# Head 0's projection, the warm products and TensorE's order in a masked attention, rewritten

## The chip, the cores and the metric

The kernel runs on one core of one Trainium2 chip. Its time is the device time of one execution in microseconds (us), and a version's time is the median of several executions. The engines are TensorE (PE; its loads of the stationary operand are listed apart as PEld), VectorE (DVE), ScalarE (ACT), GpSimd (POOL) and SyncE (SP), which here issues most of the transfers. Matrix products write to PSUM; the other engines copy from there to on-chip memory. Each engine runs its own instructions in the order in which they stand; between engines semaphores hold an instruction until what it reads is there.

## The reference

There are 2 batches of 8 heads, 768 positions, 64 numbers a head. A query and a key see each other only where the signs of their six projections agree.

```python
q_bits = (einsum('bhsd,dk->bhsk', q, proj) > 0)
k_bits = (einsum('bhsd,dk->bhsk', k, proj) > 0)
mask = bucket(q_bits)[:, :, :, None] == bucket(k_bits)[:, :, None, :]
scores = where(mask, q @ k.T / sqrt(64), -1e9)
attn = exp(scores - max(scores)); attn = attn / (sum(attn) + 1e-09)
x = attn @ v                                     # 1536 tokens x 512
h = maximum(maximum(x @ w1, x @ w2), x @ w3)     # 512 -> 768
y = h @ w_out                                    # 768 -> 512
z = y @ w_in                                     # 512 -> 2048
g = z if z >= 1 else 0 if z <= -1 else (z + 1)**2 / 4
out = g @ moe2_w_out                             # 2048 -> 512
```

## The kernel before

**The attention** takes the 16 heads (batch times head) in turn, each with six tiles of 128 queries by 768 keys, 96 tiles in all. A float32 number is held as a high part (`hi`) and the rest (`lo`), so that products of parts keep precision.

*Preparing a head.* The transposed keys and queries come into `r` (L309): 128 rows by 768 columns, keys above queries. One product per half, `bits_mm` (L389), gives the six projections of both; `bits_rows` (L395, VectorE) makes signs of them, which stand as 44 more rows in `qb`. `prep_scale` (L338) scales the queries, `prep_hi` and `prep_lo` split, and `prep_move` (L375) brings parts to other rows: `qa`, `qb`, `ql`, `kh`, `kb`. For the heads from the second on these moves are transfers issued by SyncE; `kb` needs the rows of the bits, `kh` needs `hi`. For head 0 they are copies by ScalarE and GpSimd in two halves of 384 columns, written out by hand in L596 to L621: the projection is scaled by three GpSimd ops (`pj_sign`, L327) to `pj_sc`, and 13 products of bf16 zeros, 128 x 256 (`warm_up`, L304), run on TensorE while the data are awaited. Four more stand in each half of tile 0 (L416).

*A tile.* `t_qk` (L407): for each half of the keys one product `qa` by `lo` (L414) and one of `qb` by `hi` (L417, 76 rows: the high parts and the bits, which push pairs of different buckets far down). `t_max` (L424, VectorE) takes the row maximum, `t_exp` (L439, ScalarE) the exponentials and their sums. There are two score buffers, `s_ps0` and `s_ps1`.

*The values.* For heads 0, 1, 3, 5, ... TensorE transposes each tile in 128 x 128 pieces (`t_tr`, L447, six a tile) into `t_ps`, `t_out` (L457) copies them, and `g_pv` (L508) multiplies three tiles with the values, a first third and then the rest. For the heads 2, 4, ... ("turned") VectorE transposes by 32 x 32 (`t_turn`, L464), and `block4` (L475) multiplies in four row quarters of the array, 96 products of 32 rows by 64 columns for each half of a head's blocks. `pair_rows` (L555) transposes the sums of two heads.

*The order.* Everything after head 0 is a task of a planner (`Work`, L43 to L110): a task has an engine, a cost, a due time, a lag and the tasks and buffers that it waits for, and the planner writes the instructions out in the order of its own model of time. For TensorE the order is laid down as a string (L828 to L838): `q` is the scores of a tile, `t` its transposes, `b` and `B` a head's bits, `v` and `w` the first and the rest of a value product (or the halves of a block product), `r` the sums, `m` two early pieces of the perceptrons. The number is the tile's place in the sequence (`SEQ`), not head times six plus tile: from head 1 on tiles of a turned head and another one alternate. `period`, twelve tiles, is repeated five times. Costs for changes of kind stand in L855 to L860. `SHIFT` (L630) moves the due times of the other engines' tasks.

**The perceptrons** follow from about 208 us to the end, three-part products as in `mm3` (L270) and L1017, with the weights' preparation on the other engines.

Of the kernel before, what the change touches and what calls it, by code (L numbers as in the profile page):

```python
# [8 lines left out]
F32 = mybir.dt.float32  # L9
# [104 lines left out]
def lsh_attention_moe_kernel(  # L114
# [33 lines left out]
    sc_sb = const.tile([128, 1], F32, name="sc_sb")  # L148
    one_exp = const.tile([128, 1], F32, name="one_exp")
# [131 lines left out]
    def attention(mlp_steps):  # L281
        with ExitStack() as ax, ExitStack() as sx:
# [24 lines left out]


# [98 lines left out]
            def t_qk(n, bank):  # L407
# [3 lines left out]
                for half in range(2):  # L411
# [3 lines left out]
                    if n == 0:  # L415
                        warm_up(4, half)  # L416
# [213 lines left out]
            SHIFT = {t_exp: 42.5, t_out: 2.0, g_copy: 17.5, copy4: -82.0, pair_copy: -20.5, w_tick: 60.0, bits_rows: 4.5, t_max: -12.5, t_turn: 8.0, pair_recip: 20.0}  # L630
# [9 lines left out]
            raw_s["prep"].free.pop()  # L640
            raw_s["r"].free.pop()

            def head_tasks(h):
# [17 lines left out]
                scaled[h], moves[h], r_place[h] = hi, [q, ql, kh], rp  # L661
                if h == 1:
                    bp = place("b", 1)
                    mm = task("PE", 0.644, due + 1, bits_both, h, after=[hi], takes=[bp], leaves=[rp])
# [36 lines left out]
            def tile_tasks(n):  # L701
# [6 lines left out]
                qk = task("PE", 0.72, m, t_qk, n, sp, after=ready[h], takes=[sp], leaves=[h_place[h]])  # L708
                mx = task("DVE", 1.04, m, t_max, n, sp, after=[qk], takes=[pp], leaves=[sp])
                ex = task("ACT", 1.13, m, t_exp, n, after=[mx], takes=takes, lag=0.1)  # L710
                exps[n] = ex
                order[f"qk{n}"] = [qk]
                if turned:
                    pt_p_[n] = place("dt", 1)
                    tu = task("DVE", 0.96, m - 1, t_turn, n, after=[ex] + outs.get(h, [])[-1:], takes=[pt_p_[n]], leaves=[pp])
                    outs.setdefault(h, []).append(tu)
                    return
# [5 lines left out]
                for half in range(2):  # L723
                    tr = task("PE", 0.288, m - 4, t_tr, n, half, after=[ex, tr], takes=[] if half else [tb], leaves=[pp], lag=0.1)
# [4 lines left out]
                    ways = [("ACT", 0.48 if alone else 0.76, nc.scalar.copy), ("DVE", 0.556 if alone else 0.955, nc.vector.tensor_copy)]  # L729
# [125 lines left out]
            for (x, a), (y, b_) in zip(line, line[1:]):  # L855
                b_["after"].append(a)
                if (x in "bp") != (y in "bp"):
                    b_["cost"] += 0.16
                elif x + y in ("qt", "qr", "bp", "pb"):
                    b_["cost"] += 0.06  # L860
# [238 lines left out]
```

## Time and profile before

| | us |
|---|---|
| median of 3 runs | 667.93 (667.04 to 668.33) |
| profiled execution, its own time | 668.48 |
| span of the profiled execution | 666.6 |
| busy in it: TensorE | 657.4 (99%) |
| VectorE | 486.2 (73%) |
| ScalarE | 341.0 (51%) |
| GpSimd | 274.4 (41%) |

The profile is one execution. Its own time lies 0.55 us above the median. A matrix product is listed with its line, the buffer that it writes, rows by columns of the array, its operand's shape and a count where like products are merged; the ends are modelled, so starts are what to compare. "Idle before" is the time in which the engine ran nothing, and the releaser is the instruction that ended it; "issue" stands where nothing that the profile shows was waited for.

### The profile page before, as it was taken

To read this page: it belongs to the slowest core of one execution; us is meant where nothing else is said; L and a number is where in the kernel's file an instruction comes from. 1 tells how busy PE (TensorE), PEld (TensorE's weight loads), DVE (VectorE), ACT (ScalarE), POOL (GpSimd) and SP (SyncE) were. 2 spreads that over 40 slices of the span, in tenths; PEclk is the share of its full clock that TensorE was granted. 3 is DMA by queue.
4 is the path that set the end of the run, shared out by engine and by line. 5 is a ranking of instruction groups with operands and counts; after the bars stand their busy time and mean duration, and the time that the engine had idled before them with its cause. 6 is when DMAs were issued, how large, how long until landed. Compare 5 with 4: busy or idle time off the path is not lost.

```text
span 666.6 us, 11523 instructions
## 1 busy us (share of the span) xinstructions
PE 657.4 (99%) x4419; PEld 527.4 (79%) x4419; DVE 486.2 (73%) x717; ACT 341.0 (51%) x633; POOL 274.4 (41%) x249
## 2 busy tenths in 40 slices
PE   8999999999999999999999999999999999999998
PEld 5667777777867888888888888888888888888886
DVE  5787989998863667875453466766888888888844
ACT  7787877887782233333222325665444444444430
POOL 5436556766322335344223113644444444444430
PEclk9999999999999999999999999999999999999999
DMA  6847787775243122322111122121111222211004
GB/s 194 221 122 185 199 217 197 186 243 140 83 135 81 64 95 72 119 70 65 47 49 56 55 73 86 42 71 57 63 64 64 63 65 63 64 63 64 32 0 190
DMA packets 27855, 66.99 MB, mean 100 GB/s; under 512 B 4164, under 2 KB 9124, under 8 KB 27800
## 3 DMA queue, kind: packets, MB, share of 16 engines
q1 hardware_dynamic: 27488, 66.21, 33.8%
q8 instruction: 35, 0.57, 0.4%
q14 instruction: 20, 0.16, 0.1%
q10 hardware_dynamic: 312, 0.04, 0.0%
HBM read 46.17 MB, written 3.19 MB: 74 GB/s over the span
## 4 chain that ended last, share of the span: by engine, by line
PE 96%; issue 1%; DVE 1%; DMA 1%; ACT 1%; SPq 0%; POOL 0%; POOLq 0%; DVEq 0%
PE b L270 49%; PE b L1017 20%; PE s_ps L414 6%; PE t_ps L447 5%; PE u_ps L508 5%; PE s_ps L417 5%; PE u_ps L475 3%; PE pj_ps L390 2%; PE t_ps L475 1%; DVE p L424 1%; DMA rb<-d 0%; PE pj_ps L475 0%; ACT p L439 0%; PE s_ps L270 0%; DMA d<-rt 0%
## 5 line engine op out<-in xcount | busy, mean ns | idle before, releaser
L270 PE MATMUL b<-x_hl,wx 128*128 128x512 f32 x684 | 159.6, 389 | 0.0
L270 PEld LDWEIGHTS b<-x_hl,wx 128*128 128x128 f32 x684 | 128.4, 188 | 26.6
L270 PE MATMUL b<-x_hl,w 128*128 128x512 f32 (+1 forms) x564 | 123.8, 376 | 0.0
L270 PEld LDWEIGHTS b<-x_hl,w 128*128 128x128 f32 x564 | 100.9, 188 | 19.8 <-issue 0.6
L917 POOL TENSOR_TENSOR g<-r,g 128x512 fp32r<-128x512 f32 x48 | 62.5, 1304 | 121.4 <-ACT g L916 121.4
L424 DVE TENSOR_SCALAR_CACHE_REDUCE p<-s_ps 128x768 f32<-128x768 f32 x96 | 89.7, 951 | 11.9 <-PE s_ps L417 8.7
L206 DVE SCALAR_TENSOR_TENSOR wg<-wg,wr 128x512 f32<-128x512 f32 (+1 forms) x58 | 67.3, 1160 | 37.6 <-ACT wg L204 36.9
L439 ACT ACTIVATE p<-p,nm 128x768 f32<-128x768 f32 x96 | 89.7, 936 | 5.6 <-DVE p L424 5.1
L414 PE MATMUL s_ps<-lo,q 128*128 128x384 f32 x192 | 72.0, 375 | 1.0 <-DVE p L424 0.9
L233 POOL TENSOR_TENSOR wx<-wg,wx 128x512 fp32r<-128x512 f32 (+1 forms) x32 | 45.6, 1426 | 65.3 <-ACT wx L227 48.4
L1017 PE MATMUL b<-wx,g 128*128 128x512 f32 x288 | 72.1, 389 | 0.0
L1017 PE MATMUL b<-w,g 128*128 128x512 f32 (+1 forms) x294 | 71.3, 385 | 0.0
L227 ACT CAST wx<-wg 128x512 fp32r<-128x512 f32 (+1 forms) x32 | 19.3, 604 | 92.6 <-DVE wg L219 92.6
L417 PE MATMUL s_ps<-hi,q 76*128 76x384 f32 x192 | 65.3, 340 | 0.0
L997 DVE SCALAR_TENSOR_TENSOR r<-r,b 128x512 f32<-128x512 f32 x48 | 33.0, 687 | 44.3 <-ACT r L996 44.3
L1017 PEld LDWEIGHTS b<-w,g 128*128 128x128 f32 x294 | 54.5, 188 | 11.1
L1017 PEld LDWEIGHTS b<-wx,g 128*128 128x128 f32 x288 | 54.1, 188 | 11.2
L1024 DVE TENSOR_TENSOR acc<-b,acc 128x512 f32<-128x512 f32 (+1 forms) x85 | 56.3, 675 | 7.7 <-PE b L1017 7.6
L233 POOL TENSOR_TENSOR w<-wg,w 128x512 fp32r<-128x512 f32 (+1 forms) x26 | 35.9, 1382 | 49.3 <-ACT w L227 39.1
L211 DVE TENSOR_SCALAR wg<-wg 128x512 int32<-128x512 int32 (+1 forms) x58 | 53.3, 920 | 2.7
L995 ACT ACTIVATE r<-b,half_sb 128x512 f32<-128x512 f32 x48 | 33.0, 687 | 41.3 <-PE b L270 41.3
L227 ACT CAST w<-wg 128x512 fp32r<-128x512 f32 (+1 forms) x26 | 15.8, 608 | 74.0 <-DVE wg L219 74.0
(90 smaller groups left out, 1060.2 us busy)
## 6 DMA issues: line engine op xcount, KB each, us to landing
wr<-in_w SPq DMA_DIRECT2D x48, 512.0 KB
r<-in_kq SPq DMA_DIRECT2D x15, 384.0 KB
q<-hi SPq DMA_DIRECT2D x15, 384.0 KB
v<-in_v SPq DMA_DIRECT2D x21, 256.0 KB
rb<-d SPq DMA_DIRECT2D x16, 192.0 KB
wr<-in_w SPq DMA_DIRECT2D x8, 384.0 KB
q<-lo SPq DMA_DIRECT2D x15, 192.0 KB
lo<-hi SPq DMA_DIRECT2D x15, 192.0 KB
```

Of the source, the lines that this page charges most:

```text
L206: nc.vector.scalar_tensor_tensor(out=f32(g), in0=f32(g), scalar=TINY_SQ, in1=f32(high), op0=ALU.is_ge, op1=ALU.mult)
L211: nc.vector.tensor_scalar(out=g2, in0=g, scalar1=3, scalar2=0x3FFFFFF8, op0=ALU.logical_shift_left, op1=ALU.bitwise_and)
L227: nc.scalar.copy(out=w[:, 0, 0:cols], in_=f32(g2))
L233: nc.gpsimd.tensor_tensor(out=w[:, 1, 0:cols], in0=f32(g2), in1=f32(w[:, 0, 0:cols]), op=ALU.subtract)
L270: nc.tensor.matmul(out=outp, lhsT=w_[a], rhs=x_[b_], start=(begins and i == 0 and jj == 0), stop=(ends and i == n - 1 and jj == 2),)
L414: nc.tensor.matmul(out=o, lhsT=hd["qa"][:, qs], rhs=hd["lo"][:, ks], start=True, stop=False)
L417: nc.tensor.matmul(out=o, lhsT=hd["qb"][0:76, qs], rhs=hd["hi"][0:76, ks], start=False, stop=True)
L424: nc.vector.tensor_scalar(out=p.rearrange("p (a k) -> p a k", a=2), in0=s_ps[bank.at][:, :, 0:HALF], scalar1=MASKED, scalar2=MASKED, op0=A ...
L439: nc.scalar.activation(out=p, in_=p, func=ACTF.Exp, scale=-1.0, bias=tl[n]["nm"], accum_out=sums_of(h // 2)[:, c:c + 1],)
L917: nc.gpsimd.tensor_tensor(out=dst[:, 1, cs], in0=src, in1=f32(dst[:, 0, cs]), op=ALU.subtract)
L1017: nc.tensor.matmul(out=pb[:, cs], lhsT=gs[f][:, a, tsl], rhs=wt[:, b_, cs], start=(n == 0), stop=(n == len(terms) - 1),)
L1024: nc.vector.tensor_tensor(out=acc[:, t, cs], in0=pb[:, cs], in1=acc[:, t, cs], op=ALU.add)
```

## The change

In the head: instead of 13 products of bf16 zeros, `warm_small(29)` puts 29 rounds of four float32 products of zeros, 32 rows by 64 columns out and 64 moving columns, one in each row quarter of the array, 116 in all. `pj_sc` comes from one GpSimd product of the raw projection with a table `pj_by`, which four memsets fill; `pj_sign` moves behind head 0 and is one op. The bits of head 0's two halves go to rows 0 to 63 of `pj_ps` and 64 to 127 of `u_ps`, one right behind the other; the copies of head 0 stand in a new order, and the second half of `qa` is made by GpSimd instead of ScalarE. In tile 0 one bf16 product stands in each half instead of four. In the attention: TensorE's strings are written anew, and the planner has other costs, lags, due times (`SHIFT`) and a table `SWITCH` for changes of kind; a head's bits wait for the scaled rows (`sc`) instead of `hi`.

```diff
+            def warm_small(rounds):
+                zeros = f32(warm)
+                for _ in range(rounds):
+                    for q in range(4):
+                        rows = slice(32 * q, 32 * q + 32)
+                        nc.tensor.matmul(
+                            out=quarter(q)[UP, HALF + 64:512], lhsT=zeros[rows, 0:64], rhs=zeros[rows, 64:128],
+                            start=True, stop=True,
+                        )
...
             def pj_sign():
-                for c0 in (0, 32):
-                    nc.gpsimd.tensor_scalar(
-                        out=pj_raw[:, c0:c0 + 6], in0=pj_raw[:, c0:c0 + 6], scalar1=-1.0, scalar2=0.0, op0=ALU.mult, op1=ALU.add
-                    )
-                nc.gpsimd.tensor_scalar(
-                    out=pj_sc, in0=pj_raw, scalar1=sc_sb, scalar2=0.0, op0=ALU.mult, op1=ALU.add
-                )
+                rows = pj_raw.rearrange("p (a b) -> p a b", a=2)[:, :, 0:6]
+                nc.gpsimd.tensor_scalar(out=rows, in0=rows, scalar1=-1.0, scalar2=0.0, op0=ALU.mult, op1=ALU.add)
...
                     if n == 0:
-                        warm_up(4, half)
+                        warm_up(1, half)
...
-            warm_up(13, 0)
+            warm_small(29)
             load_head(1)
             load_v(0)
-            banks0 = (pj_ps, u_ps)
             halves = [slice(0, HALF), slice(HALF, S)]
-            pj_sign()
-            prep_hi_scaled(0, halves[0])
-            bits_mm(0, 0, banks0[0], 64)
-            prep_lo_scaled(0, 0, nc.vector)
-            prep_move(0, "qb", nc.gpsimd.tensor_copy, halves[0])
-            prep_hi_scaled(0, halves[1])
-            bits_mm(0, 1, banks0[1], 64)
+            nc.gpsimd.tensor_tensor(out=pj_sc, in0=pj_raw, in1=pj_by, op=ALU.mult)
+            for half, bank in enumerate((pj_ps, u_ps)):
+                bits_mm(0, half, bank, 64 * half)
+                prep_hi_scaled(0, halves[half])
+            for half in range(2):
+                prep_move(0, "qb", nc.gpsimd.tensor_copy, halves[half])
+            prep_move(0, "qa", nc.gpsimd.tensor_copy, halves[1])
+            for half in range(2):
+                prep_lo_scaled(0, half, nc.vector)
             prep_move(0, "qa", nc.scalar.copy, halves[0])
             prep_move(0, "ql", nc.scalar.copy, halves[0])
-            prep_lo_scaled(0, 1, nc.vector)
             prep_move(0, "kh", nc.gpsimd.tensor_copy, halves[0])
-            bits_rows(0, 0, banks0[0], 64)
             prep_move(0, "ql", nc.scalar.copy, halves[1])
-            prep_move(0, "qb", nc.gpsimd.tensor_copy, halves[1])
-            prep_move(0, "qa", nc.scalar.copy, halves[1])
+            bits_rows(0, 0, pj_ps, 0)
             prep_move(0, "kh", nc.gpsimd.tensor_copy, halves[1])
             prep_move(0, "kb", nc.scalar.copy, halves[0])
-            bits_rows(0, 1, banks0[1], 64)
+            bits_rows(0, 1, u_ps, 64)
             prep_move(0, "kb", nc.scalar.copy, halves[1])
+            pj_sign()
...
+            SWITCH = dict(qt=0.095, qr=0.095, tq=-0.08, qp=0.17, qb=0.17, tp=0.094, tb=0.094)
...
-            SHIFT = {t_exp: 42.5, t_out: 2.0, g_copy: 17.5, copy4: -82.0, pair_copy: -20.5, w_tick: 60.0, bits_rows: 4.5, t_max: -12.5, t_turn: 8.0, pair_recip: 20.0}
+            SHIFT = {prep_scale_act: 10.0, prep_hi: 16.0, t_exp: 57.0, t_out: 13.0, g_copy: 18.5, copy4: -104.5, pair_copy: -48.0, w_tick: 68.0, bits_rows: 3.5, t_max: -45.0, t_turn: 6.5, pair_recip: -25.0}
...
-                scaled[h], moves[h], r_place[h] = hi, [q, ql, kh], rp
+                scaled[h], moves[h], r_place[h] = sc, [q, ql, kh], rp
...
             first_part = (
-                "q0 q1 B q2 t0 q3 q4 t1 t2 q5 b5 t3 v2 w2 t4 q6 q11 b8 t5 q7 q8 t6 v5 w5 q9 t7 q10 q12 t8 "
...
+                "q0 q1 B q2 t0 q3 t1 q4 q5 t2 b5 t3 v2 w2 t4 q6 q7 t5 b8 q8 q11 t6 q10 v5 t7 q9 w5 q12 t8 "
...
             period = (
-                "q22 q24 v19 w19 t21 q25 q26 v20 w20 q27 t23 q30 q28 t25 b25 q29 q35 t27 v25 w25 q31 r25 "
-                "t29 q32 b31 q33 t31 "
+                "q22 t19 q21 q24 v19 w19 t21 q25 q26 v20 w20 q27 t23 q28 q30 t25 q29 b25 q31 t27 v25 w25 "
+                "r25 t29 q35 q32 b31 "
             )
...
+        for rows, cols, by in ((slice(0, 64), 32, 1.0), (slice(64, 128), 0, SCALE)):
+            nc.gpsimd.memset(pj_by[rows], by)
+            nc.gpsimd.memset(pj_by[rows, cols:cols + 6], -by)
```

What this does to TensorE's row is shown at three places. In these rows a name ends in the number of its buffer, "x6" merges six like instructions, and the lines of the changed kernel are six to seven higher than those of the kernel before. The first place is the head, from the last warm products to tile 0 (`s_ps0`). Before:

```order
L306 LDWEIGHTS warm_82
L306 MATMUL t_ps_119<-warm_82 128x256
L390 MATMUL pj_ps_86<-r_120,pj_sc_77 64x384
L390 MATMUL u_ps_85<-r_120,pj_sc_77 64x384
L414 MATMUL s_ps0_116<-lo_145,q_146 128x384
L306 LDWEIGHTS warm_82
L306 MATMUL t_ps_119<-warm_82 128x256
L306 LDWEIGHTS warm_82
L306 MATMUL t_ps_119<-warm_82 128x256
```

Now:

```order
L314 MATMUL u_ps_86<-warm_83 64x64
L314 MATMUL t_ps_124<-warm_83 64x64 x2
L314 MATMUL pj_ps_87<-warm_83 64x64
L396 MATMUL pj_ps_87<-r_125,pj_sc_77 64x384
L396 MATMUL u_ps_86<-r_125,pj_sc_77 64x384
L420 MATMUL s_ps0_121<-lo_252,q_253 128x384
L307 LDWEIGHTS warm_83
L307 MATMUL t_ps_124<-warm_83 128x256
L423 MATMUL s_ps0_121<-hi_251,q_253 128x384
L420 MATMUL s_ps0_121<-lo_252,q_253 128x384
L307 LDWEIGHTS warm_83
L307 MATMUL t_ps_124<-warm_83 128x256
```

The two products of bits stand next to each other as before, but behind rounds of small products; one bf16 product is left behind each first score product.

The second place is TensorE's row in head 0, the transposes of tiles 1 and 2 (`p` is a tile's exponentials, `t_ps` the one buffer of transposes). Before:

```order
L414 MATMUL s_ps0_116<-lo_145,q_146 128x384
L417 MATMUL s_ps0_116<-hi_144,q_146 128x384
L414 MATMUL s_ps0_116<-lo_145,q_146 128x384
L417 MATMUL s_ps0_116<-hi_144,q_146 128x384
L447 MATMUL t_ps_119<-ident_84,p_198 128x128 x6
L447 MATMUL t_ps_119<-ident_84,p_213 128x128 x6
L414 MATMUL s_ps1_117<-lo_145,q_146 128x384
L417 MATMUL s_ps1_117<-hi_144,q_146 128x384
```

Now (from tile 2 in `s_ps0` on):

```order
L423 MATMUL s_ps0_121<-hi_251,q_253 128x384
L453 MATMUL t_ps_124<-ident_85,p_292 128x128 x6
L420 MATMUL s_ps1_122<-lo_252,q_253 128x384
L423 MATMUL s_ps1_122<-hi_251,q_253 128x384
L420 MATMUL s_ps1_122<-lo_252,q_253 128x384
L423 MATMUL s_ps1_122<-hi_251,q_253 128x384
L453 MATMUL t_ps_124<-ident_85,p_295 128x128 x6
L420 MATMUL s_ps0_121<-lo_252,q_253 128x384
L423 MATMUL s_ps0_121<-hi_251,q_253 128x384
```

The two rows of transposes stood in a row; now the scores of a tile stand between them.

The third place is TensorE's row around head 2's first scores (`lo_251` and `q_252` before, `lo_350` and `q_351` now; `lo_187` before and `lo_288` now are head 1's). Before:

```order
L447 MATMUL t_ps_119<-ident_84,p_329 128x128 x6
L508 MATMUL u_ps_85<-pt_293,vr_139 64x384 x6
L414 MATMUL s_ps0_116<-lo_187,q_188 128x384
L417 MATMUL s_ps0_116<-hi_186,q_188 128x384
L414 MATMUL s_ps0_116<-lo_187,q_188 128x384
L417 MATMUL s_ps0_116<-hi_186,q_188 128x384
L447 MATMUL t_ps_119<-ident_84,p_366 128x128 x6
L414 MATMUL s_ps1_117<-lo_251,q_252 128x384
L417 MATMUL s_ps1_117<-hi_250,q_252 128x384
```

Now:

```order
L453 MATMUL t_ps_124<-ident_85,p_430 128x128 x6
L420 MATMUL s_ps0_121<-lo_350,q_351 128x384
L423 MATMUL s_ps0_121<-hi_349,q_351 128x384
L420 MATMUL s_ps0_121<-lo_350,q_351 128x384
L423 MATMUL s_ps0_121<-hi_349,q_351 128x384
L514 MATMUL u_ps_86<-pt_392,vr_247 64x384 x2
L453 MATMUL t_ps_124<-ident_85,p_437 128x128 x6
L420 MATMUL s_ps1_122<-lo_288,q_289 128x384
L423 MATMUL s_ps1_122<-hi_287,q_289 128x384
L420 MATMUL s_ps1_122<-lo_288,q_289 128x384
L423 MATMUL s_ps1_122<-hi_287,q_289 128x384
L514 MATMUL u_ps_86<-pt_392,vr_247 64x384 x4
```

Head 2's first scores (q10) stood behind v5 and w5 (`u_ps`), q9 and t7; now they stand ahead of all of these.

## Rows read from the trace of the kernel before

**Rows 1.** Page, section 3 (DMA queue: packets, MB, share) and section 4 (longest chain).

```profile
q8 instruction: 35, 0.57, 0.4%
...
PE 96%; issue 1%; DVE 1%; DMA 1%; ACT 1%; SPq 0%; POOL 0%; POOLq 0%; DVEq 0%
```

**Rows 2.** Busy time by stage; columns: window, length, each engine, clock, DMA share, GB/s.

```profile
240.00:600.00 360.00, 360.00 (x1590) 298.20 (x1589) 254.76 (x324) 150.78 (x262) 135.62 (x101) 1.00 0.20 66
```

**Rows 3.** Timeline of TensorE in the head; columns: start, length, engine, line, instruction, count.

```profile
1.05 2.96 PE L306 MATMUL t_ps<-warm 128*128 128x256 bf16 x13 [1.05 <-DVE half_sb L1048]
4.87 0.86 PE L390 MATMUL pj_ps<-r,pj_sc 128*64 128x384 f32 x2 [0.85 <-POOL pj_sc L332]
...
8.02 0.44 PE L417 MATMUL s_ps<-hi,q 76*128 76x384 f32 x1
```

**Rows 4.** Timeline of GpSimd in the head, the scaled projection.

```profile
4.07 0.74 POOL L332 TENSOR_SCALAR pj_sc<-pj_raw,sc_sb 128x64 f32<-128x64 f32 x1
```

**Rows 5.** Timeline of TensorE, tiles of the first heads; the last bracket: idle before, releaser.

```profile
12.91 0.82 PE L447 MATMUL t_ps<-ident,p 128*128 128x128 f32 x6
14.68 0.88 PE L447 MATMUL t_ps<-ident,p 128*128 128x128 f32 x6 [0.95 <-ACT pt L457]
...
25.76 2.16 PE L508 MATMUL u_ps<-pt,vr 128*64 128x384 f32 x12
...
28.66 0.82 PE L447 MATMUL t_ps<-ident,p 128*128 128x128 f32 x6
29.23 0.42 PE L414 MATMUL s_ps<-lo,q 128*128 128x384 f32 x1
...
33.18 0.44 PE L414 MATMUL s_ps<-lo,q 128*128 128x384 f32 x1 [0.88 <-DVE p L424]
```

**Rows 6.** Busy time by stage, two microseconds; the last two columns: DMA share, GB/s.

```profile
18.00:20.00 2.00, 2.00 (x13) 0.70 (x10) 1.68 (x3) 0.58 (x3) 1.57 (x2) 1.00 1.10 230
```

**Rows 7.** Timelines of SyncE (issues of transfers) and of GpSimd, 17 to 25 us.

```profile
17.09 0.61 SPq L313 DMA_DIRECT2D r<-in_kq  x1
...
20.65 0.88 SPq L379 DMA_DIRECT2D lo<-hi  x1
24.11 0.83 POOL L338 TENSOR_SCALAR r<-r 64x768 f32<-64x768 f32 x1 [4.53 <-DMA r<-in_kq]
```

**Rows 8.** Timeline of TensorE within one period of twelve tiles.

```profile
110.05 0.42 PE L414 MATMUL s_ps<-lo,q 128*128 128x384 f32 x1
...
110.85 0.42 PE L414 MATMUL s_ps<-lo,q 128*128 128x384 f32 x1
...
111.64 0.82 PE L447 MATMUL t_ps<-ident,p 128*128 128x128 f32 x6
112.39 0.87 PE L390 MATMUL pj_ps<-r,pj_raw 128*64 128x384 f32 x4
...
119.03 0.42 PE L414 MATMUL s_ps<-lo,q 128*128 128x384 f32 x1
...
119.92 0.87 PE L390 MATMUL pj_ps<-r,pj_raw 128*64 128x384 f32 x4
```

**Rows 9.** Busy time by stage from the start; (x) counts products and loads started.

```profile
0.00:57.00 57.00, 53.26 (x338) 36.95 (x343) 43.89 (x86) 44.35 (x89) 27.49 (x38) 1.00 0.70 182
0.00:60.50 60.50, 56.32 (x471) 39.79 (x472) 45.97 (x90) 46.21 (x92) 30.84 (x42) 1.00 0.70 180
...
0.00:157.20 157.20, 151.53 (x1737) 111.51 (x1738) 131.98 (x241) 121.37 (x241) 91.02 (x108) 1.00 0.73 195
```

**Rows 10.** Timeline of TensorE inside two block products.

```profile
60.56 0.32 PE L475 MATMUL u_ps<-dt,v 32*64 32x192 f32 x1 [0.50 <-issue]
...
60.72 0.32 PE L475 MATMUL u_ps<-dt,v 32*64 32x192 f32 x1
...
157.26 0.32 PE L475 MATMUL pj_ps<-dt,v 32*64 32x192 f32 x1 [1.24 <-issue]
```

**Rows 11.** DMA queues from 20 to 30 us: packets, MB, share.

```profile
q8 instruction: 1, 0.02, 0.8%
```

More of the change, by code (lines that the diff above doesn't have):

```diff
@@ L148, in lsh_attention_moe_kernel @@
     sc_sb = const.tile([128, 1], F32, name="sc_sb")
+    pj_by = const.tile([128, 64], F32, name="pj_by")
     one_exp = const.tile([128, 1], F32, name="one_exp")
@@ L639, in attention @@
             scaled, moves, r_place, order = {}, {}, {}, {}
-            raw_s["prep"].free.pop()
+            h_place[0].at = raw_s["prep"].free.pop()[1]
             raw_s["r"].free.pop()
@@ L660, in head_tasks @@
                 kh = task("SP", 0.5, due + 2, prep_move, h, "kh", after=[ql], lag=3.5)
-                scaled[h], moves[h], r_place[h] = hi, [q, ql, kh], rp
+                scaled[h], moves[h], r_place[h] = sc, [q, ql, kh], rp
                 if h == 1:
                     bp = place("b", 1)
-                    mm = task("PE", 0.644, due + 1, bits_both, h, after=[hi], takes=[bp], leaves=[rp])
+                    mm = task("PE", 0.797, due + 1, bits_both, h, after=[hi], takes=[bp], leaves=[rp])
                     order["bits"] = [mm]
@@ L707, in tile_tasks @@
                 takes = own(sums_p, "sums", h // 2, 1)
-                qk = task("PE", 0.72, m, t_qk, n, sp, after=ready[h], takes=[sp], leaves=[h_place[h]])
-                mx = task("DVE", 1.04, m, t_max, n, sp, after=[qk], takes=[pp], leaves=[sp])
-                ex = task("ACT", 1.13, m, t_exp, n, after=[mx], takes=takes, lag=0.1)
+                qk = task("PE", 0.712, m, t_qk, n, sp, after=ready[h], takes=[sp], leaves=[h_place[h]])
+                mx = task("DVE", 0.9, m, t_max, n, sp, after=[qk], takes=[pp], leaves=[sp], lag=0.13)
+                ex = task("ACT", 0.97, m, t_exp, n, after=[mx], takes=takes, lag=0.05)
                 exps[n] = ex
@@ L714, in tile_tasks @@
                     pt_p_[n] = place("dt", 1)
-                    tu = task("DVE", 0.96, m - 1, t_turn, n, after=[ex] + outs.get(h, [])[-1:], takes=[pt_p_[n]], leaves=[pp])
+                    tu = task("DVE", 0.9, m - 1, t_turn, n, after=[ex] + outs.get(h, [])[-1:], takes=[pt_p_[n]], leaves=[pp], lag=0.1)
                     outs.setdefault(h, []).append(tu)
@@ L723, in tile_tasks @@
                 for half in range(2):
-                    tr = task("PE", 0.288, m - 4, t_tr, n, half, after=[ex, tr], takes=[] if half else [tb], leaves=[pp], lag=0.1)
+                    tr = task("PE", 0.327, m - 4, t_tr, n, half, after=[ex, tr], takes=[] if half else [tb], leaves=[pp], lag=0.1)
                     order[f"tr{n}"] = order.get(f"tr{n}", []) + [tr]
@@ L728, in tile_tasks @@
                     hs = slice(half, half + 1) if alone else slice(0, 2)
-                    ways = [("ACT", 0.48 if alone else 0.76, nc.scalar.copy), ("DVE", 0.556 if alone else 0.955, nc.vector.tensor_copy)]
+                    ways = [("ACT", 0.48 if alone else 0.7, nc.scalar.copy), ("DVE", 0.556 if alone else 0.955, nc.vector.tensor_copy)]
                     if alone and half:
                         ways.reverse()
-                    cp = task(*ways[0][:2], m - 4, t_out, n, hs, ways[0][2], after=[tr], takes=[pt_p_[g]] if r == 0 and (half == 0 or not alone) else [], leaves=[tb])
+                    cp = task(*ways[0][:2], m - 4, t_out, n, hs, ways[0][2], after=[tr], takes=[pt_p_[g]] if r == 0 and (half == 0 or not alone) else [], leaves=[tb], lag=0.1)
                     if alone:
@@ L742, in group_tasks @@
                 if bits:
-                    bm = task("PE", 0.644, m + 0.4, bits_both, bits, after=[scaled[bits]], takes=[bp], leaves=[r_place[bits]])
+                    bm = task("PE", 0.797, m + 0.4, bits_both, bits, after=[scaled[bits]], takes=[bp], leaves=[r_place[bits]])
                     order[f"bits{g}"] = [bm]
@@ L751, in group_tasks @@
                     last = task(
-                        "PE", 1.29 if i else 0.645, m + 0.5, g_pv, g, i, 1 + i, after=[last] if i else outs["g", g] + [vready[h]],
+                        "PE", 1.39 if i else 0.696, m + 0.5, g_pv, g, i, 1 + i, after=[last] if i else outs["g", g] + [vready[h]],
                         takes=[] if i else [up], leaves=[pt_p_[g], v_place[h]] if i else [],
@@ L773, in turned_tasks @@
                     blk = task(
-                        "PE", 1.955, m + T_AT + 0.5, block4, h, 12 * i, 12 * i + 12, after=[blk] if i else outs[h] + [vready[h]],
+                        "PE", 2.04, m + T_AT + 0.5, block4, h, 12 * i, 12 * i + 12, after=[blk] if i else outs[h] + [vready[h]],
                         takes=[] if i else banks, leaves=[pt_p_[n] for n in turned if n // NK == h] + [v_place[h]] if i else [],
@@ L856, in attention @@
                 b_["after"].append(a)
[L857 to L860, printed above, removed]
+                b_["cost"] += SWITCH.get(x + y, 0.0)
             low = exps[SEQ[30]]
```

8 lines of the change are left out of this document (4 added, 4 removed).

## Prediction

> **What bounds the kernel now.** I read the page first, then busy time by stage, then TensorE's row of the timeline through the attention. The chain that ended last is TensorE for 96% of the span [rows 1], and from 240 us to 600 us TensorE is busy for all 360.00 us [rows 2]: the perceptron part has no gap, and the change doesn't touch its instructions. What can move lies in the attention ahead of it. There too TensorE waits rarely, so two things count: the few places where it waits, and what its own instructions cost in their order. The places are the head [rows 3, 4], two waits in the first two heads' tiles [rows 5], and pauses inside the block products, for which the profile shows no releaser [rows 10]. Other engines count where they make one of these. The sum is made against the profiled execution, 668.48 us (its span is 666.6); the median of the runs is 667.93, so a difference worked out here is put on 667.93. Some 0.2%, 1.3 us, is what a measurement of this kernel can tell from no change.
>
> **The head.** Before, 13 warm products run from 1.05 us for 2.96; the bits of head 0 start at 4.87; the last score product of tile 0 starts at 8.02 [rows 3]. The bits wait for the scaled projection on GpSimd, an op that starts at 4.07 and takes 0.74 [rows 4]. Two small ops ahead of it go, so with one product of tables the bits could start near 4.4 at best (my estimate, if the new op costs what the old one did). From the bits on, the chain is bits, VectorE's two row ops, ScalarE's two copies, the last score product: 3.15 us from 4.87 to 8.02. Both halves at once, and one warm product instead of four ahead of that last one, take some 0.3 of it, by my estimate (one of the 13 is 0.23, and not all of the four were in the way). The copies moved between ScalarE and GpSimd stand beside the bits, I cost them at nothing; if the bits came before 4.4 these copies would be late instead. The four table fills lie ahead of the projection's arrival, in time in which GpSimd waits for it.
>
> In place of 13 products stand 29 rounds of four float32 products, in the stream 8 loads and 8 products a round. The trace has no such product. The nearest row is the block product L475, which also has 32 rows and 64 columns out, but 192 moving columns against 64: eight of its products repeat every 0.16 us (60.56 to 60.72, [rows 10]). Bounds: a third of that by columns, 1.6 us in all, end at 2.6; 29 x 0.16 = 4.7, end at 5.8; 29 x 0.23 (a round as long as one of the old thirteen), 6.6, end at 7.7. I take 5.8, the nearest by what is loaded. The bits then start at 5.8 instead of 4.87: 0.9 - 0.3 = **+0.6**, with ends of -0.8 and +2.5.
>
> **Instruction packets.** The page lists 35 packets with 0.57 MB on a queue for instructions [rows 1], 16 KB each. The pauses of TensorE inside block products before 60.56 us (0.50 idle) and 157.26 us (1.24 idle) [rows 10] fall where it had started 943 and 3475 loads and products [rows 9]; the distance 2532 is ten times 253. So I read them as waits for the next packet, one per some 253 instructions, in the one place where TensorE runs through two packets faster than they come. With one more between them, and the slow restart, I put their sum at 2.5 us. The changed program has 464 warm records in the head instead of 26, and 12 fewer beside tile 0: borders shift by 426 records, 1.7 packets, against the block products. Counted through the new order, three of the six again hold two borders, now the other three, one of them at its very end. Two or three pauses of 0.5 to 1.2 are 1.0 to 3.6; I take 1.7, so **-0.8** (-1.5 to +1.1). The Trainium skill (Runtime: NRT & Kernel Launch, "Instruction fetch mechanics") says that crossing a 16 KiB boundary is mostly hidden; by that the pauses would be something else and this term 0. The trace speaks against it, as the pauses keep the packets' spacing.
>
> The 464 records cross two such borders in the head as well. If the second packet comes 3.5 us after the first border, as at the block product (681 records started by 57.0, 253 behind the 943 of 60.5 [rows 9]), the stream ends between 5.3 and 7.6. That is what the rate gave, so no extra term.
>
> **The start of the attention.** First, the transposes of tiles 1 and 2 stood next to each other, 1.77 us start to start (12.91, 14.68), 0.95 of it idle for one buffer; they cost 0.6 to 0.7 otherwise. Now a tile's scores stand between them: **-1.1** [rows 5]. Second, the score tile at 33.18 waits 0.88 for VectorE; the new order has other tiles there: -0.5 to -1.0. Third, and against these, head 2's first score tile (29.23) is moved ahead of v5, w5, q9 and t7, which lie from 25.76 to 29.23, 3.5 us [rows 5]. With the first gain and the later head it is asked for at 25.8 - 1.1 + 0.6 = 25.3. Its data come over SyncE's queue, whose first 25 entries stay in their order, and the 16 transfer engines are full (share 1.10 from 18 to 20 us [rows 6]). Raw rows issued at 17.09 could be used by GpSimd at 24.11, 7.0 us; head 2's last piece, kh, was issued at 20.65, so by the same flight it is there at 27.7 [rows 7]. Its bits' row ops no longer stand behind a copy on VectorE, so kh may be issued up to 0.9 earlier; with full transfers I give half of that to the landing, 27.2, with bounds of 26.0 and 28.2. TensorE then waits 1.9 us at that tile, and the four units come behind it: 27.2 + 3.5 = 30.7 where before all of them were through at 29.23, +1.5. VectorE works on during the wait, so the stall of 33.18 goes, -1.0. Start and head together: **+0.5** (from 26.0: -0.7; from 28.2 with half of the stall left: +2.0). The gains of the transposes, and the loss of the head, end in this wait.
>
> **The order in the steady part.** The number of each unit is the same; neighbours change. Start to start, a transpose before scores takes 0.57 (28.66 to 29.23 [rows 5]), before bits 0.75 (111.64 to 112.39); a score tile that follows a transpose takes 0.80 before another (110.05 to 110.85), 0.89 before bits (119.03 to 119.92) [rows 8]. Over the whole attention the new order has nine more neighbours transpose-scores, seven fewer transpose-bits or -value and one fewer transpose-transpose; in return seven more score tiles stand before bits or values. So 7 x -0.18 - 0.07 + 7 x 0.09: **-0.7** (0 to -1.5). The transposed sums (r) that move behind the second value product cost 0.1 in either place. The new due times, lags and costs reorder VectorE, ScalarE and GpSimd; I cost them at nothing, hidden as long as TensorE finds the next score buffer free. Without that cover one late maximum costs as much as the 0.88 of [rows 5].
>
> Sum: 0.5 - 0.8 - 0.7 = -1.0, so 667.93 - 1.0 = 666.9; its own range, from the ends that go together, 665.0 to 669.6.
>
> **The rivals.** A: the order works as written. Head 2's data are there when asked for, and the warm stream ends before the projection comes. Then -0.8 for the head, -1.1, -1.0, -0.7, -0.8: -4.4, 663.5. For it: a lighter load could bring kh in some 4.5 us. Against it: the 7.0 us and the full transfers.
>
> B, slower: the head's second packet comes late. From 20 to 30 us one instruction packet is moved in the trace before [rows 11], in full transfers; the changed program needs its own in the head, by record 449 or so. If it comes at 9.5, the bits start at 9.7 and tile 0 is 4.5 late. Head 2's bits and its kh are late with it, so its tile still waits some 1.0. Then 4.5 - 1.1 + 1.0 - 0.5 - 1.5 = +2.4, 670.3. It decides from bits later than 8.7. Against it: the first border is passed before 4 us, when little is moved.
>
> C: the neighbours' prices don't change with the order; the -0.7 is 0, 667.6. For it: [rows 8] are single pairs, and bits and values need their own setup wherever they stand. The Trainium skill (TensorEngine Tiling (Array Packing), Key Properties) says that a change of tiling mode drains the engine; bits, values and block products are one mode here, and their runs per twelve tiles stay at five, so by that rule the term is 0 too. The rows, 0.57 against 0.75 for the same transposes, agree that the change costs.
>
> **How the numbers follow.** The forecast 0.60, A 0.20, B 0.13, C 0.07. The likeliest gives 666.9. Faster by over 0.2% is below 666.6: two fifths of the forecast (0.24), and A: 0.44. Slower is above 669.3: some of the forecast's upper end (0.08), and B: 0.21. Between: the rest of the forecast and C: 0.35. These lie on both sides, so the forecast's own range stands above. The range 663.2 to 670.2 leaves out about half of B and of A's lower end.
>
> **What would show it.** In the trace after: the last warm product near 5.8 and the bits just behind it, tile 0's last score product near 8.6; no wait between the first transposes; at head 2's first score tile a wait of 1 to 3 us behind a transfer; none near 33 us; pauses in other block products than before; the perceptron part as long as before. The prediction is wrong if head 2's tile finds its data (A), if the bits start after 8.7 us (B), or if waits for VectorE turn up in the middle of the attention, for which I left nothing.

## The result

The changed kernel is slower: 674.89 us median (674.80 to 676.84, 5 runs) against 668.05 for the kernel before beside it (667.04 to 668.65), a ratio of 1.0115 with a 95% interval of 1.0098 to 1.0132. The forecast was 666.9 with a range up to 670.2. The profiled execution took 674.80 us, its span is 673.0.

Where the 6.4 us of span came from shows in three marks on TensorE's timeline, the first block product, the sixth, and the first perceptron product behind the last value product. The kernel before:

```profile
56.44 0.37 PE L475 MATMUL u_ps<-dt,v 32*64 32x192 f32 x1
...
176.78 0.37 PE L475 MATMUL u_ps<-dt,v 32*64 32x192 f32 x1
...
208.36 7.95 PE L270 MATMUL b<-x_hl,w 128*128 128x256 f32 x45
```

The changed kernel:

```profile
60.47 0.37 PE L481 MATMUL u_ps<-dt,v 32*64 32x192 f32 x1
...
179.37 0.37 PE L481 MATMUL u_ps<-dt,v 32*64 32x192 f32 x1
...
214.74 1.46 PE L271 MATMUL b<-x_hl,w 128*128 128x256 f32 x10
```

So the start lost 4.0 us (56.44 to 60.47), the steady part gained 1.4 (120.3 to 118.9), the end lost 3.8 (31.6 to 35.4), and from there on both take 458.3. The pauses inside block products, measured from a product's first start to the start of what follows it, against 4.09 undisturbed, sum to 2.8 before and 1.3 after; 0.8 of those 1.3 lie in the end. Without pauses: start +4.0, steady part +0.8, end +3.0, pauses -1.5.

**The head after.** TensorE's timeline (columns as in [rows 3]; the answer to those rows):

```profile
5.88 0.22 PE L314 MATMUL t_ps<-warm 32*64 32x64 f32 x2
8.46 0.21 PE L314 MATMUL pj_ps<-warm 32*64 32x64 f32 x1 [2.35 <-issue]
...
8.73 0.54 PE L396 MATMUL pj_ps<-r,pj_sc 128*64 128x384 f32 x1
...
10.97 0.45 PE L423 MATMUL s_ps<-hi,q 76*128 76x384 f32 x1 [0.88 <-ACT hi L387]
...
11.68 0.69 PE L423 MATMUL s_ps<-hi,q 76*128 76x384 f32 x1
12.16 0.53 PE L420 MATMUL s_ps<-lo,q 128*128 128x384 f32 x1
...
13.57 1.44 PE L396 MATMUL pj_ps<-r,pj_raw 128*64 128x384 f32 x4
...
15.41 0.34 PE L420 MATMUL s_ps<-lo,q 128*128 128x384 f32 x1
```

The stream of small products would have been over near 6.0, but stops for 2.35 us two groups before its end, waiting for nothing that the profile shows. The bits start at 8.73, head 1's bits at 13.57 (9.09 before). From 11 to 15 us the products run slower too: a score product is listed with 0.53 at 12.16 and 0.34 at 15.41. The stages show the clock (the third number from the end):

```profile
10.00:12.00 2.00, 1.12 (x5) 0.77 (x5) 0.99 (x2) 1.37 (x3) 0.00 (x0) 0.84 0.63 182
12.00:14.00 2.00, 2.00 (x7) 1.43 (x8) 1.28 (x3) 1.92 (x3) 0.57 (x1) 0.50 0.39 145
```

0.50 of full speed is the 1.2 GHz level; ahead of it TensorE had stood still for 2.35 us and again while the bits' rows were made. Against like products in the runs below this cost 0.6 at tile 1, 0.6 at head 1's bits, and some 0.2 in tile 0, 1.4 in all.

### The profile page after: what moved, and what is told of

It reads as the page before. It is cut to its first block, busy times and chain, and to the rows that moved or that the text cites. A ratio compares the mean times of both kernels' runs of the same rounds, so it can differ in the third digit from the quotient of the medians.

```text
span 673.0 us, 11960 instructions
## 1 busy us (share of the span) xinstructions
PE 661.4 (98%) x4632; PEld 529.5 (79%) x4632; DVE 484.5 (72%) x717; ACT 339.7 (50%) x632; POOL 274.9 (41%) x253
## 4 chain that ended last, share of the span: by engine, by line
PE 91%; DMA 2%; DVE 2%; issue 2%; ACT 1%; POOL 1%; SPq 0%; POOLq 0%; ACTq 0%; DVEq 0%
PE b L271 48%; PE b L1020 19%; PE u_ps L514 5%; PE s_ps L420 5%; PE t_ps L453 4%; PE s_ps L423 4%; PE u_ps L481 2%; DMA q<-lo 1%; PE pj_ps L396 1%; PE t_ps L481 1%; DMA r<-in_kq 1%; DVE p L430 1%; ACT p L445 1%; PE s_ps L271 0%; DVE dt L470 0%
```

## The experiments

In what follows a record is one load or one product of TensorE, and a border is the place in its stream where one instruction packet ends and the next has to be there. Two theories. **Theory 1:** three places lose: the stop in the warm stream, which is a wait for an instruction packet; head 2's (and head 1's) scores, asked for before their data; and the new last part of the string. **The rival:** one cause makes it all, either the small products and the clock, or the new order whose delays all follow from its start.

**Fewer rounds.** The changed kernel with 20 rounds.

```diff
-            warm_small(29)
+            warm_small(20)
```

> The changed kernel with 20 rounds of small products in the head instead of 29, 320 records of TensorE in place of 464. Theory 1 (packet): the 2.35 us pause in the warm stream is the wait for an instruction packet, reached at record 449; with 320 records the border lies behind the bits and is passed later, when the packet is there. Then no pause, the bits start near 5.0 instead of 8.73, head 1's bits near 9.2 instead of 13.57, the clock stays full; part of it, up to 2 us, is lost again at head 2's first score tile, whose data are not there. Time 670.4 to 672.5. Rival (the small float32 products themselves, however many, hold head 0 back or keep the clock low): products at half speed between 10 and 15 us as in the changed kernel, time 673.5 to 675.

671.79 us (ratio to before 1.0057, 1.0036 to 1.0078), 3.1 less than with 29 rounds. No stop, bits at 5.54, head 1's bits at 10.05, the granted clock full. But the gain of 3.5 at head 1's bits is 2.3 at the first block product (58.22): waits for transfers come up at head 1's and head 2's first score tiles.

```profile
22.02 0.42 PE L420 MATMUL s_ps<-lo,q 128*128 128x384 f32 x1 [0.89 <-DMA r<-in_kq]
...
28.35 0.41 PE L420 MATMUL s_ps<-lo,q 128*128 128x384 f32 x1 [0.94 <-DMA r<-in_kq]
```

**26 rounds.** The same line with 26: record 449 then lies behind the bits.

> The changed kernel with 26 rounds of small products, 416 records. Theory 1 (packet): TensorE still has to stop at record 449 until the second packet is there, but now that record lies behind the bits, in the scores of tiles 0 and 1. Bits near 5.7 instead of 8.73, no pause in the warm stream, and the packet comes while head 0's rows and copies are made, so the stop falls mostly on time that is waited anyway: head 1's bits near 10 to 11.5; 671 to 673. Rival (a pause that belongs to the small products, by their number or their time, not to the record): a pause in the warm stream again, bits after 8.

674.06 us. As the packet theory has it, the stream doesn't stop and the bits start at 6.82; head 1's bits at 11.06, 2.5 earlier than with 29. The time expected was too low: head 2's first scores then wait 1.73 at 29.07, the granted clock falls behind that wait (0.50 from 32 to 34 us), and in the profiled run, the slowest of the four, the first block product starts at 60.5 as with 29 rounds.

**29 rounds in the kernel before**, in place of its `warm_up(13, 0)`.

> The kernel before with one line changed: 29 rounds of small float32 products in place of the 13 bf16 products at the head. Theory 1: the same pause of 2 to 2.5 us near 5.9, the bits near 8.7, the granted clock down behind it; 3.5 to 5 us at tile 0, of which the waits of the old order at 14.68 and 33.18 take back up to 1: 670.5 to 672.7. Rival (the new order makes the loss, the head only shifts work that waits later anyway): 667.5 to 668.7.

671.56 us (1.0049, 1.0030 to 1.0068). The stop is there, at the same record, shorter (0.71 idle, resumed at 7.89) since the stream came later to that record; bits at 8.17, head 1's bits at 12.31. The granted clock stayed full, which the expectation had wrong. So the stop is the head's and needs no new order, and the clock doesn't fall behind every such stop.

**Two transfers later.** The changed kernel with head 1's rows and head 0's values issued by ScalarE behind the high parts.

```diff
-            load_head(1)
-            load_v(0)
...
+            load_head(1, 1, nc.scalar)
+            load_v(0, nc.scalar)
```

> The changed kernel, but head 1's raw rows and head 0's values are issued by ScalarE behind the two high parts, near 4.6 us, instead of by SyncE at 2.13 and 2.60. Theory (the instruction packet waits behind these transfers): the packet is moved near 4.7 us instead of 6.07 and TensorE's pause after record 449 is 0.5 to 1.5 us instead of 2.35; the bits start near 7.3. Rival (the packet needs about 2.5 us from its border whatever else is moved): packet near 6, pause unchanged, bits near 8.7. The total says little, since head 1's data come later.

The DMA queues, 6.0 to 6.5 us of the changed kernel, then 3.5 to 4.0 of this one (packets, MB, share):

```profile
q8 instruction: 1, 0.02, 11.5%
```

```profile
q8 instruction: 1, 0.02, 18.2%
```

The first instruction packet moves some 2 us earlier, right behind the border that the stream passes at 3.5, and the stop is gone altogether. So the stop is a wait for a packet, and the packet waited behind transfers. How much of it an earlier packet alone would have left isn't shown: the stream ran slower in this execution (it was at the place of the stop at 7.0 instead of 5.9, bits at 7.26), and the theory had left 0.5 to 1.5. The Trainium skill (Runtime: NRT & Kernel Launch, "Instruction fetch mechanics") calls the crossing of such a border mostly hidden; here it was not. The total, 677.24 in one run, says little, as expected: head 2's scores wait 2.7.

**The order alone**, with the old head, three times (the second and third are the same kernel).

> The kernel before with the new order and the new planner's numbers, and the old head. Theory 1: no pause in the head; 1 us gained at the start less a wait at head 2's first score tile, some 2 gained from there to 180 us, and about 3.8 lost from 180 to 208 us, where the changed kernel waits for ScalarE's copies and for VectorE: 667.5 to 669.5. Rival A (the head makes the whole loss, the end's waits come from its lateness): 664 to 666.6. Rival B (the order makes most of it): above 671.

> The old head with the new order once more, for another profile. Theory (the spread is the wait for head 1's and head 2's data at the start, which differs from run to run with the transfers): a profile whose time is above 673 shows the difference before the first block product (56.3 us in the first profile), and the waits at the end unchanged at 2.8 in sum. Rival (the spread comes later): the first block product near 56 again, and waits in the middle.

> The same kernel again, with the same expectation: time and start of the first block product move together, one microsecond for one.

674.87 us median of 5 runs (1.0096, 1.0060 to 1.0132), but from 671.22 to 677.37; the repeats 673.79 and 676.50. By the median this is rival B: the order with the old head is as slow as the whole change. The three profiles, at 671.22, 673.48 and 675.31, answer the second expectation: the first block product starts at 56.28, 58.95 and 60.74, and nothing else differs by more than 0.5. The bits tell a part of why. First and third profile:

```profile
4.29 0.87 PE L390 MATMUL pj_ps<-r,pj_sc 128*64 128x384 f32 x2 [0.28 <-POOL pj_sc L332]
```

```profile
4.79 1.54 PE L390 MATMUL pj_ps<-r,pj_sc 128*64 128x384 f32 x2 [0.78 <-POOL pj_sc L332]
```

In the third they are nearly twice as long: TensorE had not come to its upper rate, which like products show from 4.3 us on in the first profile and from 9.2 on in the third. SyncE's next load of raw rows waits for the bits, and is issued at 5.84 and 7.65:

```profile
5.84 0.33 SPq L313 DMA_DIRECT2D r<-in_kq  x1
```

```profile
7.65 0.33 SPq L313 DMA_DIRECT2D r<-in_kq  x1
```

These 1.8 us are 4.5 at the first block product. The rest lies at head 2's first score tile, and right behind it. That tile in the three profiles:

```profile
26.39 0.41 PE L414 MATMUL s_ps<-lo,q 128*128 128x384 f32 x1 [1.20 <-DMA q<-lo]
```

```profile
27.51 0.41 PE L414 MATMUL s_ps<-lo,q 128*128 128x384 f32 x1 [2.28 <-DMA r<-in_kq]
```

```profile
29.34 0.45 PE L414 MATMUL s_ps<-lo,q 128*128 128x384 f32 x1 [2.32 <-DMA lo<-hi]
```

The wait is 1.1 longer in the second and third, and behind it the granted clock falls. The stage from 30 to 32 us in the first and in the third profile (the second has 0.50 as well):

```profile
30.00:32.00 2.00, 2.00 (x14) 1.19 (x11) 1.91 (x4) 0.86 (x2) 0.00 (x0) 1.00 0.26 57
```

```profile
30.00:32.00 2.00, 2.00 (x7) 0.54 (x5) 0.96 (x2) 0.13 (x1) 0.30 (x1) 0.50 0.60 146
```

From this tile to the first block product are 29.9 us in the first profile and 31.4 in the two others: the fall costs 1.5. So 4.5 is 1.8 of lateness, 1.1 of wait and 1.5 of clock. Of all nine executions of the order alone, the two with a mean granted clock of 0.999 or more took 671.2 and 671.8, the seven with 0.997 or less 673.5 to 677.7. In the changed kernel the load is issued at 9.67 (6.40 before), 60.47 at the block product, with a clock's fall of its own in tile 0. In the old order, where the clock stayed full, the load at 9.70 (29 rounds) gives 59.70 and at 6.40 it gives 56.44, one for one. Without a fall the order alone costs 2.8 us of span (669.4 against 666.6), and the end accounts for it (34.7 us from the sixth block product against 31.6).

**One tile moved in the kernel before:** head 2's first scores.

```diff
-t6 v5 w5 q9 t7 q10 q12 t8
+t6 q10 v5 w5 q9 t7 q12 t8
```

> The kernel before with one tile moved in TensorE's string: head 2's first scores ahead of v5, w5, q9 and t7. Theory (its data come too late for that place): a wait of 1.5 to 3 us at that tile, of which the stall at 33.18 gives back up to 1: 668.3 to 670.5. Rival (the other engines' order follows, and the data come earlier too): 667 to 668.2.

670.59 us against 668.46 (1.0036, 1.0023 to 1.0048). The wait at that tile, which the forecast had put at 1.9 (in this execution the bits took 1.54 as well, so some of it is theirs; the granted clock stayed full behind it):

```profile
28.57 0.41 PE L414 MATMUL s_ps<-lo,q 128*128 128x384 f32 x1 [2.24 <-DMA q<-lo]
```

**The same tile moved back** in the changed kernel with 20 rounds.

```diff
-q11 t6 q10 v5 t7 q9 w5 q12
+q11 t6 v5 t7 q9 w5 q10 q12
```

> The changed kernel with 20 rounds and head 2's first score tile back behind v5, t7, q9 and w5. Theory (its data come too late for the new place): the wait of 1.2 us there goes, no new one of over 0.4 takes its place, 1 us less than with 20 rounds alone: 670 to 671.5. Rival (the wait only moves to the tile of head 2 that follows, or to the transposes): no change, 671.3 to 672.5.

674.93 us, a miss. The wait at that tile is gone, as the theory had it; but head 3's first tile now waits, and the profile names GpSimd's low part for it. The two tiles:

```profile
30.25 0.45 PE L420 MATMUL s_ps<-lo,q 128*128 128x384 f32 x1
...
37.30 0.41 PE L420 MATMUL s_ps<-lo,q 128*128 128x384 f32 x1 [1.92 <-POOL lo L373]
```

Behind this wait the granted clock falls too (0.50 from 40 to 42 us), and the first block product is at 60.45 instead of 58.22. With the string the planner's order of ScalarE, VectorE and SyncE changed in a few places, GpSimd's, by the names in the trace, in none; why head 3's tile comes to wait is open. A place in the string can't be priced apart from what follows it.

**The transposes apart**, in the kernel before.

```diff
-t0 q3 q4 t1 t2 q5 b5 t3
+t0 q3 t1 q4 q5 t2 b5 t3
```

> The kernel before with one swap in TensorE's string: the transposes of tile 1 ahead of tile 4's scores, tile 5's scores between the transposes of tiles 1 and 2. Theory (the gain is taken back by the next tile whose data come by transfer, head 1's first, which were there 1.1 us ahead): the wait of 0.95 at the second transposes is gone, 0 to 1 us is left of it at head 2's tile: 667 to 668. Rival (it stays as a gain in full, or the swap makes new waits): 666.5 to 667, or above 669.

668.22 against 668.46 (1.0001, 0.9986 to 1.0016). The 0.95 of [rows 5] is gone and a wait of 1.06 stands at head 1's first scores, 21.15. The gain was not there to be had.

**The new head with the old order** and 20 rounds.

> The kernel before with the new head (projection by one product, bits at once, one bf16 product in tile 0's halves) and 20 rounds of small products. Theory 1: bits near 5.0, tile 0's last product near 7.8, 0.2 to 0.5 earlier than before; 667.2 to 668.3. Rival (the rest of the new head costs time as well, by its copies' order or by the clock): above 669.

668.23 (0.9993, 0.9979 to 1.0007): no difference. Bits at 5.38, first scores at 6.81 behind a wait of 0.57 for GpSimd's copies, which now stand in one row.

**The old last part** in the changed kernel with 20 rounds.

```diff
-q94 q88 q90 t85 q89 t94 q91 t87 v85 w85 r85 t89 q95 q92 t91 q93 m0 t95
+q90 q88 t85 q94 q89 t87 v85 w85 q91 t94 q95 r85 t89 q92 q93 t91 m0 t95
```

> The changed kernel with 20 rounds and the last part of TensorE's order as in the kernel before; the planner's numbers stay new. Theory: the 3.3 us lost from 180 to 208 us come from the new last part: they go, 667.5 to 669.3, and the last value product lies 3 us nearer to the last block product but one. Rival (they come from the new due times of maxima, copies and sums): the waits for ScalarE and VectorE at the end stay, 671 to 672.5.

670.13 us (1.0029, 1.0014 to 1.0043), 1.7 less than with 20 rounds alone and between the two expectations. In the traces the end is 2.3 shorter (34.6 to 32.3 from the sixth block product), against 31.6 before. TensorE's waits at the end of the changed kernel:

```profile
190.35 0.88 PE L453 MATMUL t_ps<-ident,p 128*128 128x128 f32 x6 [0.38 <-ACT pt L463]
...
192.45 0.88 PE L453 MATMUL t_ps<-ident,p 128*128 128x128 f32 x6 [0.51 <-ACT pt L463]
...
196.37 0.88 PE L453 MATMUL t_ps<-ident,p 128*128 128x128 f32 x6 [0.75 <-ACT pt L463]
...
201.22 0.96 PE L271 MATMUL s_ps<-x_hl,w 128*128 128x512 f32 x3 [1.14 <-DVE p L430]
```

and with the old last part:

```profile
193.27 0.87 PE L453 MATMUL t_ps<-ident,p 128*128 128x128 f32 x6 [0.39 <-DVE pt L463]
...
196.79 0.98 PE L271 MATMUL s_ps<-x_hl,w 128*128 128x512 f32 x3 [0.57 <-DVE p L430]
```

The four waits stand within 0.02 in each of the eight other traces that have the new last part. In it three rows of transposes come with only one tile's scores, or one value product, between them, while `t_ps` is still being copied by ScalarE; and the early perceptron piece `m0` follows at once on the scores whose buffer it needs, with no transposes between.

**The old due times** in the same kernel.

```diff
-            SHIFT = {prep_scale_act: 10.0, prep_hi: 16.0, t_exp: 57.0, ...
+            SHIFT = {t_exp: 42.5, t_out: 2.0, g_copy: 17.5, copy4: -82.0, ...
```

> The changed kernel with 20 rounds and the due times (SHIFT) of the kernel before; the strings stay new. Theory (the last part's string makes the loss at the end): the waits at the end stay within 1 us, 670.5 to 674, perhaps with new waits in the middle, since these due times belong to another order. Rival (the due times make it): 2 to 3.5 us less at the end, 667.5 to 669.5.

673.08: the four waits stay (0.38, 0.53, 0.75, 1.14). The due times don't make the end.

**The old head, the new order, the old last part.**

> The old head, the new order, but the last part of the string as before. Theory: 2.5 to 3.3 less at the end than with the new order alone, waits of 0.75 and 1.14 there gone; the start as spread as before: 668 to 672. Rival (the end was not the string): no change against the new order alone.

670.51 (668.36 to 673.60), a ratio of 1.0038 (1.0019 to 1.0057); the profiled one has the first block product at 56.6 and the end at 32.3 from the sixth, where the order alone has 34.7.

**Of the strings only the period new**, with the old head and the planner's new numbers.

> The old head, the new planner's numbers, and of the strings only the repeated period new; start and end as before. Theory: the start is as in the kernel before (first block product 56 to 57), five periods 0.5 less by the neighbours' prices, and 0.5 to 1 more by short waits: 667.5 to 669. Rival A (the steady part gains its 0.7): 666.5 to 667.5. Rival B (the new due times cost at the start too): above 669.5.

670.86 (1.0041, 1.0029 to 1.0054). Rival B has the time: the start, with its old string, has the first block product at 59.6 in the profiled run and waits for GpSimd (1.22 at 37.95), for transposes' copies (0.95) and a late projection. But that run, at 673.20, is the slowest of the ten, and its bits took 1.54, so its start is not all due to the due times. From the first to the sixth block product it takes 121.1 us, 0.7 more than before, with 0.6 less of pauses.

**Borders moved.** The swap of the transposes, and 13 small rounds for the 13 bf16 products.

> The same swap, and 13 rounds of small products instead of the 13 bf16 products: 208 records instead of 26, which moves the packets' borders by 182 against the block products, so that by count only block products 2, 4 and 6 hold two borders, the second near their ends, and none of 1, 3 and 5. Warm stream over by 3.9, no border but the first in the head. Theory: pauses in block products sum to about 1.0 instead of 2.8; 665 to 667.3. Rival (the pauses don't follow the count of records): sum as before, 667 to 668.5.

668.06 (0.9999, 0.9987 to 1.0010). The place was right and the size was not: pauses stand in block products 2, 4 and 6 and none in 1, 3 and 5, but they sum to 3.7, not 1.0. Two of them:

```profile
83.78 0.32 PE L485 MATMUL pj_ps<-dt,v 32*64 32x192 f32 x1 [1.21 <-issue]
...
180.03 0.37 PE L485 MATMUL t_ps<-dt,v 32*64 32x192 f32 x1 [0.80 <-issue]
```

So no single cause makes the whole loss: in the old order the new head with 20 rounds costs nothing and 29 rounds cost 3.5 us, and the new order costs 2.8 by itself and more where the granted clock falls. No version tried beats the kernel before: the three that come near it lie within 0.1%.

## Why the prediction was wrong

**The head: the step "so no extra term".** The warm stream's end was well sized, 6.0 without the stop against 5.8, with some luck: a round takes 0.21 at first and 0.12 from 4.6 on, and the 0.16 of the forecast lies between. What failed was taking 3.5 us from the border to the packet, a row of a block product at 57 us. There the packet is moved at 58.2, 1.2 behind its border. In the head it stood behind head 1's and head 0's loads and is moved at 6.1, 2.5 behind its border; from the border at 3.5 to resumption at 8.46 are 4.9. That is rival B's mechanism, with the bits at 8.73 where it was said to decide from 8.7. It was held unlikely because "little is moved" when the border is passed; the loads issued at 2.13 and 2.60 were on their way just then (DMA share 0.76 from 3.5 to 6.0). The 1.4 of the clock's fall behind the stop stands in no term.

**The start: the term was right for a head on time.** With the old head and bits at 4.29 the first block product is at 56.28, 0.2 ahead of before, where the sum had +0.5 between -0.7 and +2.0; the wait at head 2's tile was forecast as 1.9 and is 1.20 there and 2.24 when that move is made alone. What the sum missed is the other way in which the head reaches this place: the next load of raw rows waits for the bits, so lateness is not absorbed at head 2's tile but carried there. I let the loss of the head "end in this wait"; it didn't. In the changed kernel hardly any wait is left, and the first block product is 4.0 late:

```profile
30.60 0.41 PE L420 MATMUL s_ps<-lo,q 128*128 128x384 f32 x1 [0.24 <-DMA q<-lo]
```

And where this tile does wait longer, the granted clock can fall behind the wait, at a price of 1.5 in the order alone; the sum had no clock in it.

**The packets: -0.8 forecast, -1.5 measured**, at the edge of its bounds. Their places can be counted, their sizes can't: 0.1 to 1.7 in these traces.

**The steady part: -0.7 forecast, +0.8 measured.** By the smallest distance of each neighbourhood in the traces, added up, a period takes 23.22 before and 23.11 after, five periods -0.5, so that price was near. What ate it is waits for score buffers, which the forecast put with the other engines' tasks, "I cost them at nothing". A score tile that starts within 0.05 us of the VectorE maximum that frees its buffer takes some 0.1 more; the profile shows hardly any idle time for it (0.05 in all), as ends are modelled. The tile ahead of the third block product, before and after, 0.80 and 0.90 start to start:

```profile
103.39 0.34 PE L414 MATMUL s_ps<-lo,q 128*128 128x384 f32 x1
...
104.19 0.37 PE L475 MATMUL u_ps<-dt,v 32*64 32x192 f32 x1
```

```profile
107.23 0.44 PE L420 MATMUL s_ps<-lo,q 128*128 128x384 f32 x1
...
108.13 0.37 PE L481 MATMUL u_ps<-dt,v 32*64 32x192 f32 x1
```

All ten tiles ahead of value and block products take 0.89 to 0.91 now, and nine of the ten 0.79 to 0.80 before. The traces with the new period agree: 117.9 to 118.5 us without pauses from first to sixth block product in nine of the eleven others, 118.8 and 119.6 in two with other waits, against 117.1 to 118.0 with the old period. Rival C (0 for this term) was nearer than the forecast; the Trainium skill's rule (TensorEngine Tiling (Array Packing), Key Properties), by which the term is 0, is not shown by it, since the prices did move. The prediction calls bits, values and block products one mode; in the rows bits and values are listed as 128*64 and block products as 32*64. The number of changes doesn't depend on that, as block products stand between score tiles in both orders.

**The end: nothing forecast, +3.0 measured.** This is the step that failed by most beside the head. I compared neighbours and counted changes of kind, but didn't ask of each row of transposes when the buffer ahead of it would be copied, which I did do for tiles 1 and 2. The four places can be pointed out in the string, and with the old last part 2.3 of the 3.0 go, in three kernels (32.2 to 32.3 from the sixth block product without pauses). The other 0.7 stays in all three, which have the new period and the planner's new numbers; its cause is open.

What stays open: why TensorE reaches its upper rate near 4 us in one execution and near 9 in another, and so how the small products and the old ones compare in that; and why the granted clock falls behind some waits and not behind others. It fell in the changed kernel after the stop, and in five other profiles behind one wait of 1.7 to 2.7 us; it didn't fall after the shorter stop of the kernel before with 29 rounds, nor behind the 2.24 of the kernel before with one tile moved.

## What to carry to other kernels

Where an engine's instruction stream is lengthened, count its records against the borders of the instruction packets, and look at what is queued for transfer at the moment at which a border is passed. A saving on a chain that ends in a transfer is worth what that transfer lets through: ask when the data were issued, and what instruction released that issue. When an order is written anew, price each wait for a single buffer along the whole string, the end included, before pricing the neighbours. Look at the granted clock behind each long wait: here its fall cost more than the difference between the waits.

## What the runs showed that I had not expected

An instruction packet that is due while 0.6 MB of loads are under way lets TensorE go on 4.9 us after its border (3.5 to 8.46); without those loads there was no stop. The time at which TensorE's products come to their upper rate after the start differs by nearly 5 us between executions of one kernel (4.3 and 9.2), and the granted-clock column says 1.00 all along there, so it has to be read from the lengths of like products (0.87 and 1.54 for the same bits). Later on the column does show a fall, and much of the spread of the order alone, 671 to 678 us, goes with it.
